# Two transformer layers on one core: the first chunk's output projections, two token tiles behind q and two behind k

## The chip, the cores and the metric

The program runs on one core of one Trainium2 chip. Times are device microseconds (us) of one execution. In the profile PE is TensorE (matmul), PEld its weight loads, DVE VectorE, ACT ScalarE, SP SyncE, which issues the DMAs.

## The reference, cut to what matters

Two layers, each an attention block A and a gated feed-forward block B, on 2048 tokens of width 1024, all bf16:

```python
x = x + _A_ref(_layernorm(x), wqkv, wo)   # 32 heads of 32; each token sees 8 keys, 2 apart
x = x + _B_ref(_layernorm(x), w1, w3, w2) # (silu(x@w1) * (x@w3)) @ w2, inner width 3584
# ... and both once more, with the same weights
```

In A, each token has eight logits in each head (its query with the keys at distances 0, 2, ..., 14), a softmax over them, and a weighted sum of eight values, followed by the output projection with `wo`.

## The kernel before

The tokens go in 4 chunks of 512 (4 token tiles of 128). TensorE runs in the order in which the program emits (it alone is scheduled by hand). The order on the other engines is chosen when the program is built, by a scheduler with a clock of its own; each engine then runs its list in that order.

The attention itself, scores and weighted sums, is done on VectorE, in tiles of 256 tokens, two to a chunk:

```python
def t_scores(l, tcx):                       # cut
    psm = wk.tile([P, W, TCH], BF16, name="psm")
    for w_ in range(W):                     # 8 products, each with a tree of adds
        pr = scr.tile([P, KT, TCH], BF16, name="pr", tag="scr")
        nc.vector.tensor_tensor(pr[:], qT[:], kT[:, :, k0:k0 + TCH], op=ALU.mult)   # L228
        tree_sum8(pr, psm[:, w_, :])                                                # L174-176
    nc.vector.transpose(psmT[...], psm[...])                                        # L233
    nc.vector.reduce_sum(L[...], psmT[:], axis=AX.X)                                # L235
    ...                                     # maximum, exp, sum, normalise; then At   L260
def t_values(l, tcx):                       # 8 times: product with At (L273), tree of adds -> oT
def o_tile(l, n):                           # output projection of one token tile: 16 matmuls
    for hh in range(2):
        ps = bank("po")                     # one of the 8 PSUM banks
        for t in range(KT): nc.tensor.matmul(ps[:], lhsT=oT[...], rhs=wo[...], ...)
        with hp(): nc.vector.tensor_tensor(xs, xs, ps[:], op=ALU.add)               # L287
def ln_half(key, c, r):                     # layernorm of two token tiles, high priority
    ...  # 4 bn_stats (L124), 2 bn_aggr, sqrt on ACT, reciprocal (L129), 2 tensor_scalar -> xn (L133)
    nc.sync.dma_start_transpose(out=xnT[:, :, j * P:(j + 1) * P], in_=xn[:])        # L135, per tile
```

The feed-forward of a chunk multiplies the transposed `xnT` (both halves of it) with `w1` ("gate", pg, L305) and `w3` ("up", pu, L309), makes `hT = silu(pg) * pu` on ACT and DVE (DVE: L314), in 16 and then 12 products, and after each of these two splits multiplies `hT` with `w2` (acc, L327). The first such matmul group needs the 16th (or 12th) product at its end, so TensorE waits there if DVE is behind.

The main loop, with the part that is changed, and what follows it:

```python
for c in range(NCH):
    for which in range(3):                  # q, k, v of chunk c for layer 1
        q_part(0, c, which)                 # 64 matmuls, copied out by ACT
        ...
        if c == 3 and which == 0:
            o_tile(0, 0)
        if c == 3 and which == 1:
            o_tile(0, 1)
            ln_half(("B", 0, 0), 0, 0)
            o_tile(0, 2)
            o_tile(0, 3)
            ln_half(("B", 0, 0), 0, 1)
    ...
for u, (l, c) in enumerate(units):          # the feed-forwards, chunk by chunk
    attend(l2, c2)                          # t_scores and t_values of the next chunk, on DVE
    ...                                     # inserts: its o_tiles and layernorms inside b_stage
    q = u + 3                               # cut: a condition
    ins[8] = [lambda: ln_chunk(("Q", lq, cq), cq)]   # layernorm for the next layer's q
    b_stage(l, c, ins)
```

Of the kernel before, what the change touches and what calls it, by code (L numbers as in the profile page):

```python
# [15 lines left out]
def kernel(  # L16
# [22 lines left out]
    NCH = S // CH  # L39
# [39 lines left out]
    def bank(name):  # L79
        return psum.tile([P, 512], FP32, name=name, tag="mm")  # L80
# [27 lines left out]
    def hp():  # L108
        return tc.high_priority(offset=BOOST)
# [3 lines left out]
    def ln_half(key, c, r):  # L113

        with hp():
            if key not in xnTs:
                xnTs[key] = xtp.tile([P, KT, CH], BF16, name="xnT")
            xnT = xnTs[key]
            st = small.tile([P, 2, 2, 6], FP32, name="st")
            mv = small.tile([P, 2, 2], FP32, name="mv")  # L120
            for i in range(2):
                n = c * TPC + 2 * r + i
                for hh in range(2):
                    nc.vector.bn_stats(st[:, i, hh, :], x_sb[:, n, hh * 512:(hh + 1) * 512])  # L124
                nc.vector.bn_aggr(mv[:, i, :], st[:, i, :, :])
            sd = small.tile([P, 2], FP32, name="sd")
            rstd = small.tile([P, 2], FP32, name="rstd")
            nc.scalar.activation(sd[:], mv[:, :, 1], ACTF.Sqrt, bias=epst[:])
            nc.vector.reciprocal(rstd[:], sd[:])  # L129
            for i in range(2):  # L130
                j = 2 * r + i
                xn = xnp.tile([P, D], BF16, name="xn")
                nc.vector.tensor_scalar(xn[:], x_sb[:, c * TPC + j, :], mv[:, i, 0:1], rstd[:, i:i + 1],  # L133
                                        op0=ALU.subtract, op1=ALU.mult)
                nc.sync.dma_start_transpose(out=xnT[:, :, j * P:(j + 1) * P], in_=xn[:])  # L135

    def ln_chunk(key, c):
        ln_half(key, c, 0)
        ln_half(key, c, 1)
# [53 lines left out]
    def q_part(l, c, which):  # L193

        xnT = xnTs[("Q", l, c)]
        ws = wq_held[which]
        for t0 in range(0, KT, SG):
            sgt = stg.tile([P, SG, CH], BF16, name="sgt")
            for t in range(t0, t0 + SG):
                ps = bank("ps")  # L200
                for kk in range(KT):
                    nc.tensor.matmul(ps[:], lhsT=ws[kk // KH][:, kk % KH, t::KT], rhs=xnT[:, kk, :],  # L202
                                     start=(kk == 0), stop=(kk == KT - 1))
                nc.scalar.copy(sgt[:, t - t0, :], ps[:])  # L204
            nc.sync.dma_start(qkv_d[l][which][:, t0:t0 + SG, c * CH:(c + 1) * CH], sgt[:])
# [57 lines left out]
    def t_values(l, tcx):  # L263

        At = Ats[l, tcx]
        vT = qkvp.tile([P, KT, HALO + TCH], BF16, name="vT")
        load_halo(vT, l, 2, tcx * TCH)
        oT = wk.tile([P, KT, TCH], BF16, name="oT", bufs=2)
        for t in range(KT):
            tm = scr.tile([P, W, TCH], BF16, name="tm", tag="scr")  # L270
            base = vT[:, t, HALO:HALO + TCH]
            win = bass.AP(vT.tensor, base.offset, [list(base.ap[0]), [-DIL, W], [1, TCH]])
            nc.vector.tensor_tensor(tm[:], At[:], win, op=ALU.mult)  # L273
            tree_sum8(tm, oT[:, t, :])
        oTs[l, tcx] = oT

    def o_tile(l, n):

        oT, j = oTs[l, n // 2], n % 2
        for hh in range(2):  # L280
            ps = bank("po")
            for t in range(KT):
                nc.tensor.matmul(ps[:], lhsT=oT[:, t, j * P:(j + 1) * P], rhs=wo[:, t, hh * 512:(hh + 1) * 512],  # L283
                                 start=(t == 0), stop=(t == KT - 1))
            xs = x_sb[:, n, hh * 512:(hh + 1) * 512]
            with hp():
                nc.vector.tensor_tensor(xs, xs, ps[:], op=ALU.add)  # L287
# [62 lines left out]
    for c in range(NCH):  # L350
        for which in range(3):
            q_part(0, c, which)
            if which == 1 and c + 2 < NCH:
                nc.sync.dma_start(x_sb[:, (c + 2) * TPC:(c + 3) * TPC, :], xin[:, (c + 2) * TPC:(c + 3) * TPC, :])
            if which == 1 and c == 1:
                nc.sync.dma_start(wo[:], wo_v)
            if which == 0 and c + 1 < NCH:
                ln_chunk(("Q", 0, c + 1), c + 1)
            if c == 3 and which == 0:
                o_tile(0, 0)  # L360
            if c == 3 and which == 1:
                o_tile(0, 1)
                ln_half(("B", 0, 0), 0, 0)
                o_tile(0, 2)
                o_tile(0, 3)
                ln_half(("B", 0, 0), 0, 1)
            if c == 0 and which == 1:
                t_scores(0, 0)
        if c == 0:
            t_values(0, 0)  # L370
            t_scores(0, 1)
            t_values(0, 1)
# [48 lines left out]
```

## Time and profile before

| | kernel before |
|---|---|
| time, 6 runs | 1636.84 us median (1635.89 to 1637.71) |
| profiled span | 1635.4 us |
| PE busy | 99% of the span |
| DVE busy | 70% of the span |

The table of windows of the kernel before (busy us of PE, PEld, DVE, ACT, POOL, number of instructions in brackets; then granted clock, DMA share, GB/s):

```profile
160.00:196.00 36.00, 35.28 (x163) 20.84 (x161) 35.86 (x66) 7.25 (x13) 0.00 (x0) 1.00 0.72 221
201.00:206.00 5.00, 5.00 (x17) 1.96 (x16) 4.96 (x4) 1.11 (x2) 0.00 (x0) 0.66 0.98 294
206.00:340.00 134.00, 131.89 (x612) 59.66 (x611) 132.55 (x224) 24.45 (x35) 0.00 (x0) 1.00 0.50 155
340.00:510.00 170.00, 167.32 (x775) 75.36 (x773) 168.98 (x295) 34.17 (x47) 0.00 (x0) 1.00 0.57 172
510.00:640.00 130.00, 130.00 (x604) 67.71 (x603) 91.59 (x155) 31.58 (x49) 0.00 (x0) 1.00 0.73 220
```

The table of waits of TensorE (waiter, releaser, total us, times, longest) lists everything that PE waited for in the 1635 us:

```profile
PE pg L305 <- DMA xnT<-xn: 4.9, 1, 4.9
PE acc L327 <- DVE hT L314: 4.7, 3, 2.1
PE pT L162 <- DVE xn L159: 2.8, 3, 1.2
PE pw L104 <- DVE hT L99: 1.2, 1, 1.2
PE ps L202 <- ACT xnT L163: 1.1, 1, 1.1
PE ps L202 <- DVE x_sb L287: 0.7, 1, 0.7
```

The first and the last touch the change. The timeline of PE (start, duration, engine, line, operation; in brackets the idle time before and what ended it) shows where they are: the wait for the gate, the throttled group behind it (3.28 us, where a group of 8 otherwise takes 1.89), and three waits for hT.

```profile
170.73 10.52 PE L283 MATMUL po<-wo,oT 128*128 128x512 bf16 x48
181.09 5.34 PE L202 MATMUL ps<-xnT,wqkv 128*128 128x512 bf16 x24
187.09 8.85 PE L202 MATMUL ps<-xnT,wqkv 128*128 128x512 bf16 x40 [0.66 <-DVE x_sb L287]
200.80 3.28 PE L305 MATMUL pg<-xnT,w1t 128*128 128x512 bf16 x8 [4.86 <-DMA xnT<-xn]
203.87 2.23 PE L309 MATMUL pu<-xnT,w3t 128*128 128x512 bf16 x8
...
263.25 24.56 PE L327 MATMUL acc<-w2t,hT 128*128 128x512 bf16 x113 [2.11 <-DVE hT L314]
347.30 18.52 PE L327 MATMUL acc<-w2t,hT 128*128 128x512 bf16 x85 [1.86 <-DVE hT L314]
425.06 24.56 PE L327 MATMUL acc<-w2t,hT 128*128 128x512 bf16 x113 [0.75 <-DVE hT L314]
```

The timeline of DVE in the same place: the second half of the layernorm (two xn at 195.67) stands behind a score transpose and a reduce of 2.3 us each. There is no idle time in these lines.

```profile
139.79 2.31 DVE L260 STREAM_TRANSPOSE At<-AeT 128x2048 bf16<-128x2048 bf16 x1
...
181.37 2.31 DVE L233 STREAM_TRANSPOSE psmT<-psm 128x2048 bf16<-128x2048 bf16 x1
183.60 0.65 DVE L287 TENSOR_TENSOR x_sb<-x_sb,po 128x512 bf16<-128x512 bf16 x1
184.18 2.27 DVE L235 TENSOR_REDUCE L<-psmT 128x512 f32<-128x2048 bf16 x1
...
191.26 0.99 DVE L133 TENSOR_SCALAR xn<-x_sb,mv,rstd 128x1024 bf16<-128x1024 bf16 x2
195.67 1.00 DVE L133 TENSOR_SCALAR xn<-x_sb,mv,rstd 128x1024 bf16<-128x1024 bf16 x2
```

And the DMA transposes on SP's queue, in the timeline of SP:

```profile
191.82 2.65 SPq L135 DMA_TRANSPOSE xnT<-xn  x2
196.23 2.61 SPq L135 DMA_TRANSPOSE xnT<-xn  x2
```

### The profile page before, as it was taken

How to read it: one execution, taken by the hardware profiler on the slowest of the kernel's cores; microseconds unless marked ns; L12 is line 12 of the kernel's file. 1: busy time of each engine (PE TensorE's matmuls, PEld its weight loads, DVE VectorE, ACT ScalarE, POOL GpSimd, SP SyncE). 2: the span in 40 equal slices, each digit the busy share in tenths (PEclk: the TensorE clock that was granted, in tenths of full speed). 3: DMA queues.
4: the chain of work that ended last, by engine and by line, in shares of the span. 5: the costliest groups of instructions: out<-in, count | busy, mean ns of one | idle time of the engine just before them, and what ended most of it. 6: DMA issues, size and time to landing. Idle time of an engine off the chain costs nothing.

```text
span 1635.4 us, 18944 instructions
## 1 busy us (share of the span) xinstructions
PE 1616.1 (99%) x7472; PEld 800.2 (49%) x7472; DVE 1152.4 (70%) x1961; ACT 340.5 (21%) x530; POOL 1.9 (0%) x12
## 2 busy tenths in 40 slices
PE   8999899999999999999999999999999999999999
PEld 5666444444444644446444554445544444444444
DVE  4899999999999781897728977299652992332212
ACT  3333311203021320223202232022320211121110
POOL 0000000000000000000000000000000000000000
PEclk9999999999999999999999999999999999999999
DMA  9943746557546774367743686438753574256440
GB/s 297 280 132 102 220 158 195 159 151 209 183 131 180 240 235 150 106 193 245 221 142 104 199 259 200 142 104 249 255 178 119 129 232 155 90 143 205 155 129 26
DMA packets 337113, 286.32 MB, mean 175 GB/s; under 512 B 69632, under 2 KB 319488, under 8 KB 336896
## 3 DMA queue, kind: packets, MB, share of 16 engines
q1 hardware_dynamic: 337024, 285.11, 57.2%
q8 instruction: 58, 0.95, 0.2%
q14 instruction: 31, 0.25, 0.0%
HBM read 239.99 MB, written 29.36 MB: 165 GB/s over the span
## 4 chain that ended last, share of the span: by engine, by line
PE 67%; DVE 29%; issue 3%; DMA 1%; ACT 0%; DVEq 0%; ACTq 0%
PE acc L327 21%; PE pg L305 15%; PE pu L309 15%; PE ps L202 13%; DVE pr L228 5%; DVE tm L273 4%; PE po L283 3%; DVE hT L314 3%; DVE tm L174 3%; DVE pr L174 2%; DVE x_sb L287 1%; DVE st L124 1%; DVE tm L175 1%; DVE pr L175 1%; DVE L L235 1%
## 5 line engine op out<-in xcount | busy, mean ns | idle before, releaser
L305 PE MATMUL pg<-xnT,w1t 128*128 128x512 bf16 x1792 | 424.7, 380 | 4.9 <-DMA xnT<-xn 4.9
L309 PE MATMUL pu<-xnT,w3t 128*128 128x512 bf16 x1792 | 423.7, 379 | 0.0
L327 PE MATMUL acc<-w2t,hT 128*128 128x512 bf16 x1792 | 390.8, 379 | 5.1 <-DVE hT L314 4.7
L202 PE MATMUL ps<-xnT,wqkv 128*128 128x512 bf16 x1536 | 334.3, 380 | 1.8 <-ACT xnT L163 1.1
L313 ACT ACTIVATE sg<-pg 128x512 bf16<-128x512 f32 x224 | 133.4, 597 | 843.2 <-PE pg L305 831.4
L314 DVE TENSOR_TENSOR hT<-sg,pu 128x512 bf16<-128x512 bf16 x224 | 152.1, 679 | 212.2 <-PE pu L309 210.7
L305 PEld LDWEIGHTS <-w1t 128*128 128x128 bf16 x1792 | 175.5, 98 | 217.0 <-issue 6.6
L327 PEld LDWEIGHTS <-hT 128*128 128x128 bf16 x1792 | 174.8, 98 | 218.5 <-DVE hT L314 9.0
L309 PEld LDWEIGHTS <-w3t 128*128 128x128 bf16 x1792 | 175.5, 98 | 212.0 <-issue 1.0
L202 PEld LDWEIGHTS <-wqkv 128*128 128x128 bf16 x1536 | 220.5, 144 | 114.6 <-issue 3.9
L332 DVE TENSOR_TENSOR x_sb<-x_sb,acc 128x512 bf16<-128x512 bf16 x128 | 87.0, 680 | 162.2 <-PE acc L327 162.2
L228 DVE TENSOR_TENSOR pr<-qT,kT 128x2048 bf16<-128x2048 bf16 x128 | 153.1, 1210 | 51.6 <-issue 32.1
L273 DVE TENSOR_TENSOR tm<-At,vT 128x2048 bf16<-128x2048 bf16 x128 | 151.7, 1213 | 0.3
L204 ACT CAST sgt<-ps 128x512 bf16<-128x512 f32 x192 | 108.7, 588 | 184.6 <-PE ps L202 151.7
L283 PE MATMUL po<-wo,oT 128*128 128x512 bf16 x512 | 115.4, 379 | 0.0
L124 DVE BATCH_NORM_STATS2 st<-x_sb 128x6 f32<-128x512 bf16 x120 | 79.9, 681 | 18.0 <-DMA x_sb<-in_A_x_dram 17.3
L174 DVE TENSOR_TENSOR pr<-pr 128x1024 bf16<-128x1024 bf16 x128 | 85.6, 680 | 0.0
L174 DVE TENSOR_TENSOR tm<-tm 128x1024 bf16<-128x1024 bf16 x128 | 84.4, 681 | 0.0
L283 PEld LDWEIGHTS <-oT 128*128 128x128 bf16 x512 | 50.0, 98 | 60.4
L287 DVE TENSOR_TENSOR x_sb<-x_sb,po 128x512 bf16<-128x512 bf16 x64 | 43.2, 677 | 15.4 <-PE po L283 15.4
L175 DVE TENSOR_TENSOR pr<-pr 128x512 bf16<-128x512 bf16 x128 | 51.8, 415 | 0.2
L175 DVE TENSOR_TENSOR tm<-tm 128x512 bf16<-128x512 bf16 x128 | 50.3, 415 | 0.1
(169 smaller groups left out, 428.7 us busy)
## 6 DMA issues: line engine op xcount, KB each, us to landing
w1t<-in_B_w_dram SPq DMA_DIRECT2D x56, 1024.0 KB, 5.4
w3t<-in_B_w_dram SPq DMA_DIRECT2D x56, 1024.0 KB, 7.2
w2t<-in_B_w_dram SPq DMA_DIRECT2D x48, 1024.0 KB, 5.4
wqkv<-in_A_wqkv_dram SPq DMA_DIRECT2D x28, 1024.0 KB, 6.6
w2t<-in_B_w_dram SPq DMA_DIRECT2D x16, 512.0 KB, 5.1
qkv_d_0_158<-sgt SPq DMA_DIRECT2D x16, 256.0 KB, 5.3
qkv_d_1_159<-sgt SPq DMA_DIRECT2D x16, 256.0 KB, 4.4
qT<-qkv_d_0_158 SPq DMA_DIRECT2D x8, 512.0 KB, 4.0
```

The source lines that it names most:

```text
L174: nc.vector.tensor_tensor(buf[:, 0:4, :], buf[:, 0:4, :], buf[:, 4:8, :], op=ALU.add)
L175: nc.vector.tensor_tensor(buf[:, 0:2, :], buf[:, 0:2, :], buf[:, 2:4, :], op=ALU.add)
L202: nc.tensor.matmul(ps[:], lhsT=ws[kk // KH][:, kk % KH, t::KT], rhs=xnT[:, kk, :], start=(kk == 0), stop=(kk == KT - 1))
L204: nc.scalar.copy(sgt[:, t - t0, :], ps[:])
L228: nc.vector.tensor_tensor(pr[:], qT[:], kT[:, :, k0:k0 + TCH], op=ALU.mult)
L273: nc.vector.tensor_tensor(tm[:], At[:], win, op=ALU.mult)
L283: nc.tensor.matmul(ps[:], lhsT=oT[:, t, j * P:(j + 1) * P], rhs=wo[:, t, hh * 512:(hh + 1) * 512], start=(t == 0), stop=(t == KT - 1))
L305: nc.tensor.matmul(pg[:], lhsT=w1t[:, kk, fi * P:(fi + 1) * P], rhs=xnT[:, kk, :], start=(kk == 0), stop=(kk == KT - 1))
L309: nc.tensor.matmul(pu[:], lhsT=w3t[:, kk, fi * P:(fi + 1) * P], rhs=xnT[:, kk, :], start=(kk == 0), stop=(kk == KT - 1))
L313: nc.scalar.activation(sg[:], pg[:], ACTF.Silu)
L314: nc.vector.tensor_tensor(hT[:, g0 + fi - f0, :], sg[:], pu[:], op=ALU.mult)
L327: nc.tensor.matmul(acc[:], lhsT=hT[:, f - f0, j * P:(j + 1) * P], rhs=w2ts[(f - f0) // 8][:, (f - f0) % 8, :], start=(f == f0), stop=(f == ...
```

## The change

The intent: the first feed-forward cannot start before both halves of chunk 0 are projected, normalised and transposed. So tile 1 and with it the first half's layernorm move one projection earlier, behind q instead of behind k; tiles 2 and 3 stay behind k.

```diff
-            if c == 3 and which == 0:
-                o_tile(0, 0)
-            if c == 3 and which == 1:
-                o_tile(0, 1)
-                ln_half(("B", 0, 0), 0, 0)
-                o_tile(0, 2)
-                o_tile(0, 3)
-                ln_half(("B", 0, 0), 0, 1)
+            if c == NCH - 1 and which < 2:
+                o_tile(0, 2 * which)
+                o_tile(0, 2 * which + 1)
+                ln_half(("B", 0, 0), 0, which)
```

## The prediction

> **What bounds the kernel.** TensorE is busy 1616.1 of 1635.4 us (the page's first part). The table of waits has only 15.4 us of TensorE waits on other engines; the change can touch two of them: 4.86 us in which the first gate matmul waits for the DMA transpose of the normalised chunk 0 (195.9 to 200.8 us in the timeline), and 0.66 us at 186.4 us, where a v matmul waits for a PSUM bank held until VectorE adds an output projection to x. After the 4.86 us the granted clock is 0.66 from 201 to 206 us (table of windows): the first gate and up groups of 8 take 3.28 and 2.23 us where later ones take 1.89. The Trainium skill, "TensorE: Matmul & The Clock Gate", Part 1, says that an idle window of about 3.4 us puts the clock to half; this trace agrees. So about 4.9 + 0.7 + 1.7 = 7.2 us (0.44%) can be won at the very most.
>
> **What the change does.** No instruction is added or removed. On TensorE, output tile 1 (32 minus 16 = 16 matmuls, 3.45 us) moves from behind k to before k. From 181.1 us on TensorE runs the same order as before: tiles 2 and 3 still end at 177.6 and 181.1 us, then v, then the gate. On VectorE the two adds, two statistics, one aggregate, the reciprocal and the two normalisations of the first half move ahead of the transpose of the scores; its two DMA transposes then issue near 176 us instead of 191.8.
>
> **What lies on the critical path.** The gate waits for all four token tiles, so for the second half: its two normalisations run at 195.7 to 196.7 us, its transposes issue at 196.2 and 197.5 us and land 3.2 us later, at 200.8. What holds the second half back is not TensorE (tile 3 was finished at 181.1 us) but VectorE, which is busy without a gap from 160 to 197 us (timeline and windows) and runs in program order. I compared the instruction orders of the two builds: from the last value sum of chunk 0 to the second-half normalisation each VectorE operation occurs the same number of times in both. The first half's work, about 3.5 us (two adds 1.2, two statistics 1.2, aggregate and reciprocal 0.2, two normalisations 0.9 to 1.0), only goes in front of the 2.3 us score transpose and the 2.2 us reduce, which are pushed back by as much, and both still precede the second half. So the second-half xn should come at 195.7 us again, give or take 0.4, and the gate start at 200.8. The PSUM wait in v should stay: the second add of tile 2 now ends near 190.6 us (transpose 184.9 to 187.1, add to 187.8, reduce to 190.0, add), one v group wants that bank at 189.7, so about 0.9 us instead of 0.66; it is swallowed by the wait for xnT, which shrinks by as much. Net: 0 us.
>
> **Prediction.** 1636.3 us, range 1634.4 to 1638.0; faster by over 2%: 0.5%, within 2%: 99%, slower: 0.5%.
>
> **What would show it.** xnT wait at the first gate 4.4 to 5.3 us, gate starting at 200.4 to 201.2; first-half transposes near 176 us; second-half ones near 196.2; score transpose of VectorE starting near 184.9; a PSUM wait of 0.5 to 1.3 us in v; granted clock again below 1 after the wait.
>
> **What would make it wrong.** If the first half's transposes, rather than VectorE, delayed the second half, the wait shrinks and up to 5 us come back, plus the clock. If ScalarE, which now waits for the first half's variance near 172 us before it may copy k banks, fills PSUM or delays stores, a new TensorE wait of 1 to 2 us appears.

## More of the kernel before

The page of the kernel before: the busy rows of its first part, and two rows of its second, where each digit is the busy share, in tenths, of one fortieth of the span (41 us).

```profile
PE 1616.1 (99%) x7472; PEld 800.2 (49%) x7472; DVE 1152.4 (70%) x1961; ACT 340.5 (21%) x530; POOL 1.9 (0%) x12
PE   8999899999999999999999999999999999999999
DVE  4899999999999781897728977299652992332212
```

The average of DVE hides a stage: from the third slice to the thirteenth, 82 to 530 us, it is at 90% or more, with PE.

## The result

1636.96 us median of 6 runs (1635.01 to 1638.73) against 1636.84 us: ratio 1.0001, 95% interval 0.9988 to 1.0014. Ratios here and below are the mean time of one kernel's fast runs over that of the other's in the same rounds, so not quite the ratio of the medians quoted.

The waits of TensorE after the change:

```profile
PE acc L327 <- DVE hT L314: 4.8, 3, 2.2
PE pg L305 <- DMA xnT<-xn: 3.8, 1, 3.8
PE pT L162 <- DVE xn L159: 3.4, 4, 1.2
```

(Cut: the two start-up waits of 1.2 and 1.1 us, as before.)

The timeline of PE after the change, the same places:

```profile
175.36 7.07 PE L283 MATMUL po<-wo,oT 128*128 128x512 bf16 x32
182.27 13.98 PE L202 MATMUL ps<-xnT,wqkv 128*128 128x512 bf16 x64
200.08 3.41 PE L305 MATMUL pg<-xnT,w1t 128*128 128x512 bf16 x8 [3.84 <-DMA xnT<-xn]
203.33 1.89 PE L309 MATMUL pu<-xnT,w3t 128*128 128x512 bf16 x8
...
262.44 24.56 PE L327 MATMUL acc<-w2t,hT 128*128 128x512 bf16 x113 [2.19 <-DVE hT L314]
346.50 18.52 PE L327 MATMUL acc<-w2t,hT 128*128 128x512 bf16 x85 [1.86 <-DVE hT L314]
424.26 24.56 PE L327 MATMUL acc<-w2t,hT 128*128 128x512 bf16 x113 [0.75 <-DVE hT L314]
```

The timelines of DVE and of SP after the change:

```profile
139.00 2.31 DVE L260 STREAM_TRANSPOSE At<-AeT 128x2048 bf16<-128x2048 bf16 x1
...
174.22 0.99 DVE L133 TENSOR_SCALAR xn<-x_sb,mv,rstd 128x1024 bf16<-128x1024 bf16 x2
...
183.99 2.31 DVE L233 STREAM_TRANSPOSE psmT<-psm 128x2048 bf16<-128x2048 bf16 x1
186.80 2.27 DVE L235 TENSOR_REDUCE L<-psmT 128x512 f32<-128x2048 bf16 x1
194.86 1.00 DVE L133 TENSOR_SCALAR xn<-x_sb,mv,rstd 128x1024 bf16<-128x1024 bf16 x2
```

```profile
174.78 2.63 SPq L135 DMA_TRANSPOSE xnT<-xn  x2
195.43 2.64 SPq L135 DMA_TRANSPOSE xnT<-xn  x2
```

The first half is normalised and transposed 17 us earlier; the second half is not. It seems 0.8 us earlier, and so does everything after it. But this 0.8 us is there at 139 us already, long before the change: the operation that makes the attention weights At of the second attention tile starts at 139.79 us before and at 139.00 after. The start-up of the two executions differed. So I measure times from this operation, the **mark**, in every trace. Measured from the mark (a chunk's feed-forward makes 28 hT products, and they are counted on from chunk 0 into chunk 1, so the 16th, 28th, 44th and 56th end a split):

| us from the mark | before | after |
|---|---|---|
| second-half xn starts | 55.88 | 55.86 |
| gate starts | 61.01 | 61.08 |
| first hT wait ends (16th product) | 123.46 | 123.44 |
| second (28th) | 207.51 | 207.50 |
| third (44th) | 285.27 | 285.26 |
| end of the program (span minus mark) | 1495.6 | 1495.6 |

The gate wait is a microsecond shorter because PE, not DVE, came later: its first po group began at 154.64 us instead of 153.46. That this is the execution and not the change can be seen in `late` (below), whose DVE order is that of the kernel after up to 349 us: there PE was early again, and the gate waited 4.97 us, with a wait of 0.47 us for a PSUM bank in v. Why start-up varies by 1 to 2 us between executions was not studied.

### The profile page after: what moved, and what is told of

Its sections match the earlier page's. It is cut to its first block, busy times and chain, and to the rows that moved or that the text cites. A ratio compares the mean times of both kernels' runs of the same rounds, so it can differ in the third digit from the quotient of the medians.

```text
span 1634.6 us, 18944 instructions
## 1 busy us (share of the span) xinstructions
PE 1616.4 (99%) x7472; PEld 800.5 (49%) x7472; DVE 1152.3 (70%) x1961; ACT 341.3 (21%) x530; POOL 1.9 (0%) x12
## 4 chain that ended last, share of the span: by engine, by line
PE 67%; DVE 28%; issue 3%; DMA 1%; ACT 0%; DVEq 0%; SPq 0%; ACTq 0%
PE acc L327 21%; PE pg L305 16%; PE pu L309 15%; PE ps L202 12%; DVE pr L228 5%; DVE tm L273 4%; PE po L283 3%; DVE hT L314 3%; DVE tm L174 2%; DVE pr L174 2%; DVE x_sb L287 1%; DVE st L124 1%; DVE pr L175 1%; DVE tm L175 1%; DVE L L235 1%
```

## The experiments

Two accounts of where time goes had to be told apart. **A:** DVE has no gap from about 57 to 507 us and runs its list in order, so the list decides when anything that PE waits for is done, and a gain for PE at the gate is lost at the next wait for DVE. **B:** PE's waits are added up; the 5 us at the gate (and 1.5 to 1.7 us of throttled matmuls behind it) are there to be won. A rival for the gate itself was that the place of the projections, or the DMA transposes, and not DVE, holds the second half.

The "work ahead" of an operation, in the expectations, is an estimate: the sum of the durations of all DVE operations between the mark and it, in the order of the build, each with the start-to-start time that the trace of before shows. It gives 121.2, 205.5 and 283.1 us for the 16th, 28th and 44th hT product of the changed kernel, 2 us less than the table above measures (the trace of after has 2.2 to 3.1 us of idle DVE on the way, which the sum leaves out).

All results together; each kernel is compared with the kernel before in the same rounds on the same chip. The last three columns come from one profiled execution each.

| kernel | median us | ratio, 95% interval | gate wait | sum of hT waits | end from the mark |
|---|---|---|---|---|---|
| after | 1636.96 | 1.0001 (0.9988 to 1.0014) | 3.8 | 4.8 | 1495.6 |
| all_after_k | 1637.43 | 1.0003 (0.9990 to 1.0015) | 4.1 | 4.8 | 1495.3 |
| all_after_q | 1637.54 | 1.0004 (0.9992 to 1.0017) | 0 | 9.6 | 1495.9 |
| pin_after | 1636.30 | 1.0000 (0.9987 to 1.0012) | 2.1 | 6.2 | 1496.8 |
| two_more | 1641.62 | 1.0024 (1.0011 to 1.0038) | 8.2 | 4.4 | 1499.5 |
| pin_before | 1642.55 | 1.0036 (1.0024 to 1.0049) | 2.8 | 9.2 | 1501.3 |
| pin_before_xn4 | 1637.92 | 1.0002 (0.9989 to 1.0016) | 1.8 | 6.6 | 1497.2 |
| pin_after_xn4 | 1636.42 | 0.9994 (0.9981 to 1.0006) | 1.7 | 7.9 | 1496.7 |
| late | 1636.42 | 1.0001 (0.9989 to 1.0014) | 5.0 | 4.4 | 1495.9 |
| late_pin | 1635.18 | 0.9989 (0.9976 to 1.0003) | 3.5 | 3.3 | 1493.7 |
| act3_late_pin | 1634.51 | 0.9985 (0.9973 to 0.9998) | 2.8 | 4.4 | 1493.5 |
| nomax | 1638.12 | 1.0006 (0.9992 to 1.0019) | 6.4 | 3.7 | (mark moved) |
| nomax_late_pin | 1630.88 | 0.9958 (0.9946 to 0.9971) | 0.2 | 4.2 | (mark moved) |

All were correct against the reference.

One thing holds in all fourteen traces: from the end of the 56th hT product on DVE to the end of the program it is 1128.1 us, or 1129.8 us in the five kernels where PE waits about 3 us at that product and its matmuls are then throttled (pin_after, two_more, pin_before and the two with xn4). So an edit is worth what it does to the 56th product (367.5 us from the mark before and after the change, 365.6 in late_pin, 371.4 in pin_before), plus 1.7 us where the clock drops behind it. (In late and in the two without the maximum, DVE stood idle 9.7 to 14.4 us before that product, mostly waiting for PE: there PE's own work ahead of it sets the time.)

### all_after_k: all four tiles behind k

```diff
-            if c == NCH - 1 and which < 2:
-                o_tile(0, 2 * which)
-                o_tile(0, 2 * which + 1)
-                ln_half(("B", 0, 0), 0, which)
+            if c == NCH - 1 and which == 1:
+                for h_ in range(2):
+                    o_tile(0, 2 * h_)
+                    o_tile(0, 2 * h_ + 1)
+                    ln_half(("B", 0, 0), 0, h_)
```

> The changed kernel with all four projections of chunk 0 and both half normalisations behind k, so later than in either kernel. Theory A (VectorE's work ahead of an operation, in its program order, decides when it is done, because VectorE has no gap from about 60 to 507 us): the VectorE work ahead of the second-half xn is the same sum as in both kernels (56.6 us from the same starting operation), so the gate matmul starts at 200 to 201 us, wait for xnT 3.5 to 5.3 us, time within 1 us of the kernel before. Rival (place on TensorE matters: earlier is better, later is worse): tiles 0 and 1 finished up to 7 us later than before the change delay the gate by 3 us or more and the time by as much.

The gate started at 200.46 us, the same time was measured. Tile 0 and tile 1 may be projected behind q or behind k: nothing moves. The place on TensorE is not what holds the gate.

### all_after_q: all four tiles behind q

The same edit with `which == 0`.

> The changed kernel with all four projections and both half normalisations behind q. The VectorE work ahead of the second-half xn falls from 56.6 to 42.6 us, so xn comes 14 us earlier: both theories expect no wait for xnT, granted clock 1.0, gate matmul at 195 to 196.5 us. Theory A then expects the gain to be given back: VectorE's work ahead of the 16th, 28th, 44th and 56th product into hT is 120.1, 205.0, 281.9 and 365.0 us against 121.2, 205.5, 283.1 and 365.0 in the changed kernel, so the TensorE waits for hT grow from 4.8 to about 8 to 11 us in sum, and the time changes by 0 to -1 us. Rival B (the 5 us of waiting at the gate are TensorE time that is simply saved): time -5 to -7 us, waits for hT still about 4.8 us.

The gate wait is gone. These are the lines of PE's timeline of all_after_q from the gate on where it starts or waits:

```profile
195.00 1.89 PE L305 MATMUL pg<-xnT,w1t 128*128 128x512 bf16 x8
...
249.57 1.89 PE L309 MATMUL pu<-xnT,w3t 128*128 128x512 bf16 x8 [0.65 <-DVE hT L314]
258.84 0.39 PE L327 MATMUL acc<-w2t,hT 128*128 128x512 bf16 x1 [4.58 <-DVE hT L314]
261.64 26.98 PE L327 MATMUL acc<-w2t,hT 128*128 128x512 bf16 x111 [2.40 <-DVE hT L314]
346.71 18.52 PE L327 MATMUL acc<-w2t,hT 128*128 128x512 bf16 x83 [0.46 <-DVE hT L314]
```

The gate starts 55.5 us from the mark, 5.6 us earlier than after the change. Most of it is given back at the first w2 products: waits of 4.58 and 2.40 us for hT, where there was one of 2.19, leave PE 1.3 us ahead (122.15 us from the mark against 123.44). The throttled matmuls behind them (26.98 us for 111, where all_after_k takes 24.56) cost more than that. From the mark the second hT wait ends at 207.22 us against 207.50, and the program ends 0.3 us later. Theory B, which is also what both the change and the prediction's upper limit rest on, fell here (its -5 us is far outside the interval); A's number for the hT waits (8 to 11 us) held, with 9.6.

### pin_after: the score transpose behind the second half, TensorE's order untouched

```diff
+        if (l, tcx) == (0, 2):      # ahead of the score transpose; the value of psm does not change
+            nc.vector.scalar_tensor_tensor(psm[:, 0, 0:1], last_xn["B", 0, 0][:, 0:1], 0.0, psm[:, 0, 0:1],
+                                           op0=ALU.mult, op1=ALU.add)
```

(`last_xn` keeps the last xn tile of each layernorm.)

> The changed kernel with TensorE's order untouched; one 128x1 VectorE operation makes the score transpose of chunk 1 depend on the second-half xn, so the scheduler puts transpose and reduce (4.4 us) behind it. Work ahead of the second-half xn 50.7 instead of 56.6 us: xn about 189 to 190 us, gate matmul without wait at 195.5 to 196.5, clock 1.0. Theory A: work ahead of the 16th, 28th, 44th and 56th hT product 116.7, 200.4, 277.5, 362.8 (-4.5, -5.1, -5.6, -2.2): waits for hT grow by 2 to 4 us at the end of this stretch, time -2.2 us (-1 to -3.5). Rival B: -5 to -7 us. If DMA transposes and not VectorE held the gate: wait unchanged, time 0.

DVE's order alone moved the second-half xn to 51.3 us from the mark, 4.6 us earlier, with TensorE's order unchanged: DVE held the second half. The lines of DVE's and of SP's timeline of pin_after:

```profile
189.87 1.00 DVE L134 TENSOR_SCALAR xn<-x_sb,mv,rstd 128x1024 bf16<-128x1024 bf16 x2
190.44 5.12 SPq L136 DMA_TRANSPOSE xnT<-xn  x2
```

The gate came only 2.0 us earlier, though: the two transposes took 5.12 us to issue instead of 2.64, while the weight loads for the next gate tiles, issued at 184 to 187 us, were under way. And the time did not fall by the 2.2 us expected. This line of PE's timeline of pin_after shows why:

```profile
505.60 20.21 PE L332 MATMUL acc<-w2t,hT 128*128 128x512 bf16 x83 [3.04 <-DVE hT L319]
```

The 56th product, at which the kernel before waits for next to nothing, is now the tightest: a wait of 3.04 us, which ends only 0.5 us earlier from the mark than before (work ahead: -2.2, so A missed this size), and behind it 1.7 us of throttled matmuls (20.21 us where the same group takes 18.52 us in the lines above). That adds up: -0.5 + 1.7 = 1.2 us, and the end from the mark is 1.2 us later (1496.8 against 1495.6).

### two_more: 4.5 us more work on DVE

```diff
-        for w_ in range(W):
+        for w_ in (range(W) if (l, tcx) != (0, 2) else [0, 1] + list(range(W))):
```

> The changed kernel with two score products of chunk 1 computed twice (same values, result right): 4.5 us more VectorE work in the stretch. Work ahead of the second-half xn +3.1 us (59.7): gate matmul about 3 us later, at 203 to 204, wait for xnT about 7 us. Theory A: work ahead of the 16th, 28th, 44th and 56th hT product +-0, -0.5, -1.4, +2.4 us, so the later waits for hT shrink to near 0 first and the time grows by about 2 to 3 us. Rival B (the gate wait adds in full): +3.1 or more, waits for hT unchanged at 4.8.

+3.9 us from the mark and 1.0024 in time. The gate wait grew to 8.2 us, and the first and the third of the hT waits vanished. At the 56th product PE went on 2.2 us later than before (work ahead: +2.4), and 1.5 us of throttling came with the wait of 3.13 us there. So 2.2 of the 3.9 us is the term that A named, and the rest is the clock. By the two totals this run does not speak for A: 3.9 us is above its 2 to 3 and within B's "+3.1 or more", and the hT waits sum to 4.4 us, near B's 4.8. The places do: the gate came 2.9 us later, and yet PE passed the 28th product at 207.30 us from the mark, 0.2 us earlier than after the change.

### pin_before: does the change pay when DVE's order no longer holds the second half?

The pin of pin_after, put into the kernel before.

> The kernel before with the pinned score transpose: the same pair as before and after the change, with the score transpose and reduce out of the way. VectorE's work ahead of the second-half xn (50.7) and of every hT product is the same as in the pinned changed kernel. Theory A: the same time as that within 1 us (so within 1 us of the kernel before), gate at 197 to 199 us, a wait of about 3 us for hT at 505 us. Rival (the change's earlier first half pays once the second half is no longer held back): the pinned changed kernel is faster than this one by 1 us or more and this one's gate comes later.

Here A, as I had it, was wrong, and the rival was right: 1642.55 us, 5.7 us slower than the kernel before, where pin_after is level with it. The waits of DVE in pin_before, 140 to 510 us, contain one that no other kernel has:

```profile
DVE xn L134 <- DMA xnT<-xn: 4.0, 1, 4.0
```

And SP's timeline of pin_before has all four transposes in one row:

```profile
185.46 11.57 SPq L136 DMA_TRANSPOSE xnT<-xn  x4
```

Without the change, the first half's transposes come just ahead of the second's; the four take 11.57 us, the pool of normalised tiles has three buffers, so the fourth xn waits 4.0 us for one, and DVE, in order, does nothing meanwhile. My sums of work counted no waits. With the change the first half is long transposed. That is a real benefit of the change, hidden in the pair that was asked about: there the score transpose and reduce stand between the halves (before: 191.82 and 196.23 us) and no buffer is short.

### pin_before_xn4 and pin_after_xn4: a fourth buffer

```diff
-    xnp = ctx.enter_context(tc.tile_pool(name="xn", bufs=3))
+    xnp = ctx.enter_context(tc.tile_pool(name="xn", bufs=4))
-        m4 = smp.tile([P, 4, NE], FP32, name="m4")
+        m4 = smp.tile([P, 4, NE], FP32, name="m4", tag="f4")
-        e4 = smp.tile([P, 4, NE], FP32, name="e4")
+        e4 = smp.tile([P, 4, NE], FP32, name="e4", tag="f4")
-        An = smp.tile([P, W, NE], BF16, name="An")
+        An = E
```

(The other edits make room; with the fourth buffer alone the program does not build, 10.7 kB per partition being left for a pool of 12.5.)

> The pinned kernel before, which was 5.7 us slower than the kernel before, with four instead of three buffers for the normalised tiles (room made by two small softmax tiles sharing space and one written in place). Theory H: its loss is the 4.0 us in which VectorE waited, with nothing else in its order, for the first half's DMA transposes to give a buffer back. Then with a fourth buffer VectorE has no such wait, every hT product comes 4 us earlier, and the time falls to that of the pinned changed kernel, within 1.5 us of the kernel before, although four transposes in a row still take about 11 us and the gate still starts at 198 to 200 us. Rival T: the loss is the late gate (slow transposes behind the weight loads). Then the time stays 5 us above the kernel before.

> The pinned changed kernel with the same four buffers, as the control. It had no such wait of VectorE, so nothing but small shifts: within 1.5 us of the kernel before, as the pinned changed kernel was. Under theory H the two kernels of this pair differ by less than 1.5 us; under rival T this one is faster by 5 us or more.

Theory H held. With the fourth buffer DVE's wait is gone and pin_before's loss with it: 1.0002 instead of 1.0036, though the four transposes still take 10.27 us. From the mark the two kernels of the pair end 0.5 us apart (1497.2 and 1496.7), where they were 4.5 us apart with three buffers. (The timed medians are 1.5 us apart, at the very edge of what H allowed, with intervals that overlap.) Rival T is left without a case: its 5 us did not show. So what the change is worth under the pin is the price of that buffer.

### late and late_pin: take work that is not yet needed out of the stretch

```diff
+            if (l, c) == (0, 1) and lastsplit:      # in b_stage, ahead of the w2 products
+                ln_chunk(("Q", 1, 0), 0)
-            ins[8] = [lambda: ln_chunk(("Q", lq, cq), cq)]
+            if u > 1:
+                ins[8] = [lambda: ln_chunk(("Q", lq, cq), cq)]
```

> The changed kernel with one other thing moved: the layernorm of chunk 0 for layer 2's q (about 7 us of VectorE work, needed only at 525 us) is emitted behind the second half of the feed-forward's hT products of chunk 1 instead of near 370 us. VectorE's work ahead of the 16th, 28th, 44th and 56th hT product: 0, 0, -0.5, -6.7 us against the changed kernel. Theory A' (TensorE passes each of these four products no earlier than VectorE does, so the time moves only by what the tightest of them and TensorE's own work allow): gate wait 3.5 to 5, hT waits at 261 and 345 us unchanged (2.2 and 1.9), that at 424 us 0.2 to 0.8, time 0 to -0.7 us. Rival (all VectorE work moved out of the stretch counts): -6 us.

> The late layernorm of chunk 0 together with the pinned score transpose. VectorE's work ahead of the 16th, 28th, 44th and 56th hT product: -4.5, -5.1, -5.0, -6.6 us against the changed kernel, so no product holds the gain back as the 56th did in the pinned kernel alone (a wait of 3.0 us at 505 us and 1.7 us of throttled matmuls behind it). Theory A': gate as in the pinned kernel (197 to 198 us, wait about 2), hT waits at 259 and 343 us together about 3, none over 0.5 us at 505 us, clock 1.0 there, time -4 to -5 us. If the gain goes elsewhere again: a new wait of over 3 us, most likely for xnT of the late layernorm at 521 us.

`late` behaved as A said: 7 us of DVE work moved out, and the time stayed, because the 28th product is as late as ever. `late_pin` met the direction but not the size: -1.7 us in the medians (not clear of noise), -1.9 us from the mark, instead of -4 to -5. The 28th product came 3.0 us earlier, not 5.1; DVE now waits for TensorE in places (1.3 us for po, 0.6 for pu). The gate waited 3.5 us, not 2: it came 59.3 us from the mark, close to the 59.0 of pin_after, but PE was there 1.1 us sooner. Then the wait of 1.98 us before it was followed by throttled matmuls, as this line of PE's timeline of late_pin shows:

```profile
344.55 20.21 PE L334 MATMUL acc<-w2t,hT 128*128 128x512 bf16 x83 [1.98 <-DVE hT L319]
```

### act3_late_pin: a copy to ScalarE

```diff
-        nc.vector.tensor_copy(AeT[:], ...)
+        (nc.scalar.copy if (l, tcx) >= (0, 3) else nc.vector.tensor_copy)(AeT[:], ...)
```

> As the late, pinned kernel, and the four-fold copy of the attention weights (1.26 us on VectorE) runs on ScalarE from the fourth attention tile on: VectorE's work ahead of the 28th, 44th and 56th hT product -7.6, -8.7, -11.7 us against the changed kernel (-2.5, -3.7, -5.1 against the late, pinned one). Theory A': the hT waits at 343 us and later go below 0.5, time -6 to -7 us (what is left is the gate wait of about 2 and its clock). Against it: [...]VectorE's score transpose then waits for it; then the waits for hT stay and the time is only -4 to -5.

The second of the two outcomes, and smaller still: 2.1 us from the mark. The waits of DVE name the reason; the copy took 1.90 us on ACT, and four copies were waited for, at 1.2 us each, which is what the copy cost DVE before:

```profile
DVE At L265 <- ACT AeT L263: 4.9, 4, 1.4
```

### nomax and nomax_late_pin: less work on DVE

```diff
-        m4 = smp.tile([P, 4, NE], FP32, name="m4")
-        ...                                       # maximum over the 8 logits, and its subtraction
-        nc.vector.tensor_tensor(L[:], L[:], mx[:]...to_broadcast([P, W, NE]), op=ALU.subtract)
```

(The softmax is the same without its maximum as long as exp does not overflow; with these inputs the result is correct. For others that would have to be looked at.)

> The changed kernel without the subtraction of the maximum in the softmax (the four VectorE operations of the maximum, about 1.7 us in each of the 16 attention tiles; the softmax is the same without it and the result stays right). VectorE has 1.7 us less to do in each of the two tiles before the common starting operation, which so comes about 3.4 us earlier, but the scheduler fills the room with work of the next attention tile: from that start, the work ahead of the second-half xn and of the 16th, 28th, 44th and 56th hT product is +5.4, +4.8, +5.0, +6.4 and -7.4 us against the changed kernel, together +2.0, +1.4, +1.6, +3.0 and -10.8. Theory A': less VectorE work and still no gain: gate 1 to 2 us later, time +1 to +3 us. Rival (VectorE's total work in the stretch decides): time -5 us or better.

> The same cut of the softmax with the pinned score transpose and the late layernorm. Start 3.4 us earlier, and from it the work ahead of the second-half xn and of the 16th, 28th, 44th and 56th hT product -5.9, -4.0, -4.0, -4.0 and -14.0 us against the changed kernel, together -9.3, -7.4, -7.4, -7.4 and -17.4 us. Theory A': no long wait for hT is left except what TensorE's own work makes (sum below 2 us), xnT wait at the gate 0 to 2 us, time -5 to -7 us. It would be wrong if the time is not below the late, pinned kernel's (-1.8 us).

`nomax` removes work from the busiest engine of the stretch and is not faster (1.0006); the 5 us of the rival are far outside its interval. The gate came at 201.57 us and the wait at the 44th product grew to 1.83 us. A's range (+1 to +3 us) lies within the interval (-1.3 to +3.1 us), and so does no change at all. The trace has both halves of A's sum: the mark came 3.5 us earlier than after the change, and from it the 56th product ended 4.0 us later. But that product was expected 7.4 us earlier from the mark, and DVE idled 14.4 us on the way, mostly waiting for PE and ACT, against 3.6. `nomax_late_pin` has the same cut and also an order in which the room is not filled again ahead of the products: -6.9 us from its ratio (1637.29 x 0.0042), the fastest kernel here and clear of noise against the kernel before. Its gate wait is 0.2 us. The sum of its hT waits, 4.2 us, was expected below 2: PE arrives earlier now and waits again.

## Why the prediction was right

The prediction, 1636.3 us in a range of 1634.4 to 1638.0, holds; 1636.96 was measured.

- *"What holds the second half back is not TensorE ... but VectorE"*: right. The second-half xn started 55.88 and 55.86 us from the mark. all_after_k (later projections, no loss) and pin_after (DVE's order alone moves xn by 4.6 us) show it by experiment. The in-order queue that this rests on is stated by the Trainium skill, "DVE: scalar operands, raw-bit mode, write accounting and state across instructions", section 5 ("one in-order queue"); pin_after agrees, where one added dependence in DVE's list moved the xn by 4.6 us.
- *"The first half's work ... only goes in front of the score transpose and the reduce"*: right; these start 2.6 us later by the clock, 3.4 from the mark (183.99 - 139.00 against 181.37 - 139.79; expected 3.5).
- *"The PSUM wait in v should stay", about 0.9 us*: wrong. There was none. PE began its po groups 1.2 us later in this execution, so the v group came to the bank behind the add; in `late`, with PE early, it was there with 0.47 us. It made no difference, as the prediction said.
- *Gate wait 4.4 to 5.3 us, gate at 200.4 to 201.2 us*: missed, 3.84 us and 200.08 us, both by the start-up of this execution (`late`, with the same order to there: 4.97 us, and 61.04 us from the mark, where the kernel before has 61.01). Those marks should have been given relative to an operation ahead of the change.
- *Clock below 1 behind the wait*: right; the first gate group took 3.41 us instead of 1.89. The Trainium skill, "TensorE: Matmul & The Clock Gate", Part 1, calls the window by which the clock is set free-running, so that the same wait need not cost the same each time. The runs do vary (a gate wait of 2.79 us was followed by a group of 3.48 us in act3_late_pin, one of 2.78 us by a group of 1.89 us in pin_before), but no run shows the window itself.
- *"About 7.2 us can be won at the very most"* and *"up to 5 us come back, plus the clock"* if the gate were freed: wrong as a picture of what the gate is worth. all_after_q freed it by 5.6 us and won nothing. The prediction saw that DVE had no gap from 160 to 197 us, and did not look on: the stage goes on to 507 us, so what was won at the gate was lost at the products behind it (of 5.6 us, 1.3 were left at the 16th, 0.3 at the 28th, none at the 56th). The prediction was right because nothing was won at the gate either.
- *The rival in "what would make it wrong"*, the first half's transposes: not in this pair, but pin_before shows that it exists, at 4.0 us of DVE's time and 5.7 us of the program's (4.0 at the 56th product and 1.7 of clock behind it).
- *The other rival there, ScalarE filling PSUM*: its premise came true (ACT stood idle 6.03 us until the variance came at 171.44 us, then copied five banks in a row), but no new wait of TensorE appeared.

What stays open: why four transposes take 11.57 us in pin_before when a pair takes 2.6 us elsewhere. They ran while two weight tiles of 1 MB were being loaded, and a pair in the same company took 5.12 us in pin_after; no run removed the loads. (The second-half pairs of before and after, which started about 10 us or more behind the loads' issue, took 2.6 us.) The start-up variation of 1 to 2 us stays open too.

## What to carry to other kernels

When an engine runs in order and has no gap over a long stage, time is set by how much of its work stands ahead of the operations that others wait for; compare that sum, operation by operation, before believing in any wait further up, and follow the stage to its end, not to the wait that the change aims at. A sum of work is only a lower bound: a short pool (three buffers for four tiles) or a copy moved to another engine turns work into waiting of the same size. For differences below the spread of executions, measure from an operation that lies ahead of the change.

## What the Trainium skill lacked or had wrong

- "TensorE: Matmul & The Clock Gate", Part 1, puts the throttle at one or more idle windows of about 3.4 us. Here matmuls were also throttled behind idle times that the profile gives as 1.98 us (late_pin: 20.21 us for a group that otherwise takes 18.52) and 3.04 us (pin_after, the same), while the gate of pin_before, after 2.78 us, was not (1.89 us for 8). (The same part tells of a kernel throttled by frequent short idles, without their length; here it was one wait.) Waits of 2 to 3 us can cost 1.7 us on top.
- "DMA: Bandwidth & Descriptors", DMA Transpose (X-bar), says nothing on what a DMA transpose takes beside other traffic. Here a pair of 128x1024 tiles took 2.6 us to issue, and 5.12 us (pin_after) or, for two pairs, 11.57 us (pin_before) during weight loads; the loads as the cause are argued, not shown.
- No page works through the case here: an in-order engine busy 70% of the span but full from 57 to 507 us, which takes back what PE wins at one wait (5.6 us at the gate in all_after_q, none of it left at the 56th product). The nearest is "Perfetto Trace Analysis", Optimization Strategy, on kernels whose most contended engine changes over time.
